# Rearranging the warm-up products and the first transposes at the start of a fused attention and GEGLU kernel

## The chip, the core and the metric

One core of one Trainium2 chip. The metric is device time in microseconds (us) for one execution.

## The reference

```python
scores = q @ k.T / sqrt(D) + alibi bias, causal, window 128     # B, H, S, D = 8, 8, 576, 64
attn   = softmax(scores) @ v                                    # 4608 tokens x 512
g, val = attn @ w_gate, attn @ w_val                            # 512 -> 1536
out    = (gelu(g) * val) @ w_out                                # 1536 -> 512
```

## The kernel before

Attention of batch 0 comes first. From then on TensorE runs dense products of the feed-forward part almost without a break, with the attention of the later batches between them. Only the start matters here. q and k of batch 0 come in a first part (320 tokens, four heads, then four more) and a tail (256 tokens). They are transposed on TensorE and copied out of PSUM, the buffer that TensorE writes to ("untangled"). Where TensorE would stand idle, `bank()` puts products of zeros ahead of the next real work. I read them as meant to bring its clock to full rate early: in the profile before, the clock record turns to full at 4.57 us, 3.37 after the first of them, and they start 0.43 us apart until then and 0.22 afterwards.

```python
    def bank():
        ps = psum.tile([128, 512], FP32, name="ps")
        for _ in range(heat.pop()):
            nc.tensor.matmul(out=ps, lhsT=zeros[:, 0:128], rhs=zeros, start=True, stop=True)
        ...
    load_runs(0, 0, 0, 4)                 # q, k: first part, heads 0 to 3
    zeros = consts.tile([128, 512], BF16, name="zeros")
    nc.vector.memset(zeros, 0.0)
    ...                                   # ident, tmpl
    load_runs(0, 0, 4, 8); load_runs(0, 1, 0, 8)      # heads 4 to 7; the tail
    load_v(0, (0, 1, 2)); load_w(0, 256); ...
    for h in range(H):                    # mask table, ScalarE
        nc.scalar.activation(out=emask[:, h, :], in_=tmpl, func=AF.Exp, scale=-slope)

    def first(cs):                        # c: a pair of heads; w: q or k
        for w in (0, 1):
            if w and len(cs) == 2:
                keep_busy(3)
            for c in cs:
                ps = bank().bitcast(BF16)
                transpose_runs(0, 0, w, c, ps)
                untangle(dve, 0, 0, w, c, ps)

    keep_busy(8)
    first((0, 1))
    made_later()
    keep_busy(4)
    scores(0, 0, (0, 1), lambda: (keep_busy(3), first((2,)), first((3,))))
    keep_busy(2)
    scores(0, 0, (2, 3))
    scores2(0)
    keep_busy(4); rest((0, 1)); keep_busy(1); rest((2, 3))   # transposes of the tail
    sums0(0)                              # 72 short products: row sums
    values_first(...)                     # products with v, spread, then xT
    ...                                   # scores of the tail, then dense products
```

The softmax here doesn't subtract the row's maximum and nothing guards it: scores larger than these inputs give would overflow.

## Time and profile before

| | before |
|---|---|
| median of the first three runs | 357.76 us (357.66 to 359.34) |
| median of six runs, with those beside the changed kernel | 358.23 us |
| span of the profiled run | 355.6 us |
| TensorE busy | 348.9 us, 98% |
| first dense product | 18.70 us |

### The profile page before, as it was taken

The page shows a single profiled execution, that of the slowest core. Times are in us where ns is not written, and L with a number is a line of the kernel's source. Part 1 is how long each engine was busy: PE and PEld are TensorE (multiplying, and loading weights), DVE is VectorE, ACT ScalarE, POOL GpSimd, SP SyncE. Part 2 cuts the span into 40 slices and gives each one's busy share as a digit, 9 for nine tenths or more (in the row PEclk, how much of TensorE's full clock was granted, in tenths as well). Part 3 has the DMA queues.
Part 4 walks back from the last instruction along what each step waited for, and adds up shares of the span by engine and source line. Part 5 has one row for each costly group of instructions (what it writes and reads, how often), then busy time and mean ns, then how long its engine had stood idle before and what let it go on. Part 6 is the DMA issues. An engine that isn't in the chain of part 4 may idle for free.

```text
span 355.6 us, 7101 instructions
## 1 busy us (share of the span) xinstructions
PE 348.9 (98%) x2869; PEld 174.6 (49%) x2869; DVE 188.3 (53%) x327; ACT 185.8 (52%) x342; POOL 103.1 (29%) x137
## 2 busy tenths in 40 slices
PE   8999999999999999999999999999999999999996
PEld 3667545444454445445444545454444444444443
DVE  4876578344988646646455554655474404403320
ACT  5884495536877375633873297337832233313322
POOL 8943479500940275003900192004000000000000
PEclk9999999999999999999999999999999999999999
DMA  7999999999999099983997399859206020011002
GB/s 93 182 195 197 202 160 193 148 154 166 141 157 174 12 185 180 158 177 41 153 208 151 78 133 200 142 129 98 88 4 133 32 88 1 2 68 50 2 29 88
DMA packets 145632, 42.62 MB, mean 120 GB/s; under 512 B 131608, under 2 KB 138520, under 8 KB 145600
## 3 DMA queue, kind: packets, MB, share of 16 engines
q0 software_dynamic: 106368, 18.88, 69.5%
q1 hardware_dynamic: 36432, 17.31, 22.2%
q10 hardware_dynamic: 2800, 5.99, 7.8%
q8 instruction: 22, 0.36, 0.4%
q14 instruction: 10, 0.08, 0.1%
HBM read 43.65 MB, written 9.53 MB: 150 GB/s over the span
## 4 chain that ended last, share of the span: by engine, by line
PE 94%; DVE 4%; issue 0%; ACT 0%; ACTq 0%; DVEq 0%
PE ps L392 53%; PE ps L415 25%; PE ps L358 5%; PE ps L190 4%; PE ps L70 2%; PE ps L315 2%; DVE P L200 1%; DVE r L321 1%; PE ps L151 1%; PE ps L429 1%; DVE kT L161 1%; PE ps L295 1%; PE ps L282 0%; PE ps L341 0%; DVE xT L379 0%
## 5 line engine op out<-in xcount | busy, mean ns | idle before, releaser
L399 DVE TENSOR_TENSOR hT<-ps,gelu 128x512 bf16<-128x512 f32 (+2 forms) x115 | 73.7, 653 | 105.8 <-PE ps L392 90.8
L398 ACT ACTIVATE gelu<-ps 128x512 bf16<-128x512 f32 (+2 forms) x115 | 65.1, 571 | 115.3 <-PE ps L392 111.5
L392 PE MATMUL ps<-xT,wg 128*128 128x512 bf16 (+2 forms) x460 | 112.3, 367 | 0.2
L392 PE MATMUL ps<-xT,wv 128*128 128x512 bf16 (+2 forms) x460 | 112.1, 366 | 0.0
L415 PE MATMUL ps<-wo,hT 128*128 128x512 bf16 x420 | 95.7, 380 | 0.0
L197 ACT ACTIVATE P<-ps 128x512 bf16<-128x512 f32 x144 | 73.1, 631 | 7.0 <-PE ps L190 7.0
L392 PEld LDWEIGHTS <-wv 128*128 128x128 bf16 x460 | 44.6, 98 | 48.8
L392 PEld LDWEIGHTS <-wg 128*128 128x128 bf16 x460 | 43.2, 98 | 47.4 <-issue 0.5
L200 DVE TENSOR_TENSOR P<-P,emask 128x1024 bf16<-128x1024 bf16 (+1 forms) x79 | 49.1, 641 | 30.1 <-ACT P L197 29.7
L415 PEld LDWEIGHTS <-hT 128*128 128x128 bf16 x420 | 38.9, 98 | 47.9 <-issue 3.7
L99 POOL DMA_DIRECT2D vb<-in_v_dram x40 | 33.9, 887 | 13.0 <-DMA ks<-in_k_dram 6.5
L420 ACT COPY osb<-ps 128x512 f32<-128x512 f32 x31 | 18.6, 601 | 32.8 <-PE ps L415 32.8
L621 POOL COPY mark<-hT 1x2 bf16<-1x2 bf16 x4 | 0.7, 174 | 95.0 <-DVE hT L399 95.0
L368 DVE TENSOR_TENSOR xT<-ps,rb 128x256 bf16<-128x256 f32 (+1 forms) x60 | 22.9, 443 | 9.2 <-DMA rb<-rd 4.7
L321 DVE RECIPROCAL r<-ps 128x320 f32<-128x320 f32 (+1 forms) x14 | 26.6, 1931 | 1.3 <-PE ps L315 1.3
L99 POOL DMA_DIRECT2D qs<-in_q_dram x30 | 25.2, 862 | 7.2 <-DMA wo<-in_moe_w_out_dram 5.1
L99 POOL DMA_DIRECT2D ks<-in_k_dram x30 | 25.4, 899 | 2.8 <-DMA qs<-in_q_dram 2.6
L190 PE MATMUL ps<-qT,kT 64*128 64x256 bf16 (+1 forms) x384 | 22.3, 244 | 1.4 <-DVE kT L161 0.6
L190 PEld LDWEIGHTS <-kT 64*128 64x128 bf16 x384 | 13.4, 94 | 13.6 <-issue 9.5
L358 PE MATMUL ps<-P,vb 128*64 128x128 bf16 (+2 forms) x384 | 18.1, 244 | 0.0
L358 PEld LDWEIGHTS <-vb 128*64 128x64 bf16 x384 | 14.7, 110 | 5.2 <-issue 4.8
L70 PE MATMUL ps<-zeros 128*128 128x512 bf16 x25 | 8.3, 460 | 1.2 <-DVE zeros L440 1.2
(73 smaller groups left out, 117.4 us busy)
## 6 DMA issues: line engine op xcount, KB each, us to landing
out_dram<-osb SPq DMA_DIRECT2D x35, 256.0 KB, 3.9
rb<-rd ACTq DMA_DIRECT2D x10, 576.0 KB, 7.4
vb<-in_v_dram POOLq DMA_DIRECT2D x32, 128.0 KB, 7.3
qs<-in_q_dram POOLq DMA_DIRECT2D x24, 128.0 KB, 6.2
ks<-in_k_dram POOLq DMA_DIRECT2D x24, 128.0 KB, 6.6
wo<-in_moe_w_out_dram POOLq DMA_DIRECT2D x2, 768.0 KB, 18.3
wg<-in_moe_w_gate_dram POOLq DMA_DIRECT2D x2, 384.0 KB, 9.2
wv<-in_moe_w_val_dram POOLq DMA_DIRECT2D x2, 384.0 KB, 10.7
```

The lines of the kernel that those rows point to most:

```text
L99: nc.gpsimd.dma_start(out=t[lo:128, j, :].rearrange("p (h d) -> p h d", h=H), in_=src[b][:, 128 * j - 64 + lo:128 * j + 64, :].rearrange(" ...
L190: nc.tensor.matmul(out=ps[:, col:col + 128 * n].rearrange("p (n t) -> p n t", n=n), lhsT=blocks(kT, b, i, c, j, 1).rearrange("p n t -> p ( ...
L197: nc.scalar.activation(out=dst, in_=src, func=AF.Exp, scale=0.125)
L200: nc.vector.tensor_tensor(out=dst, in0=dst, in1=m, op=ALU.mult)
L321: nc.vector.reciprocal(row(b)[:, lo:hi], ps[:, 0:hi - lo])
L358: nc.tensor.matmul(out=ps[64 * i:64 * i + 64, a:e], lhsT=vb[b % 2][:, j, 64 * h:64 * h + 64], rhs=prob(b, s, c, i, j, e - a), start=(j == ...
L368: nc.vector.tensor_tensor(out=xT[:, c, b * S + lo:b * S + hi], in0=ps[:, 0:hi - lo], in1=recip[b][:, c, lo:hi], op=ALU.mult)
L392: nc.tensor.matmul(out=ps[:, 0:hi - lo], lhsT=w[:, c, 128 * f:128 * (f + 1)], rhs=xT[:, c, t0 + lo:t0 + hi], start=(c == 0), stop=(c == 3))
L398: nc.scalar.activation(out=gl[:, 0:hi - lo], in_=pg[:, 0:hi - lo], func=AF.Gelu)
L399: nc.vector.tensor_tensor(out=hid[g][:, f, lo:hi], in0=pv[:, 0:hi - lo], in1=gl[:, 0:hi - lo], op=ALU.mult)
L415: nc.tensor.matmul(out=po, lhsT=hid[g][:, f, 128 * t:128 * (t + 1)], rhs=wo[:, f, :], start=(f == 0), stop=(f == NF - 1))
L420: (nc.vector.tensor_copy if g < 2 and t < 2 else nc.scalar.copy)(out=osb, in_=po)
```

## The change

Its intent: keep TensorE on products of zeros until k is about to land, then transpose q and k back to back; let ScalarE take one of the four first copies between the fifth and the sixth row of the mask table; and make zeros smaller, so that its memset ends earlier (it took 0.27 us in the profile before).

```diff
-            nc.tensor.matmul(out=ps, lhsT=zeros[:, 0:128], rhs=zeros, start=True, stop=True)
+            nc.tensor.matmul(out=ps.rearrange("p (n x) -> p n x", n=4), lhsT=zeros,
+                             rhs=zeros.unsqueeze(1).to_broadcast((128, 4, 128)),
+                             start=True, stop=True)
...
+    zeros = consts.tile([128, 128], BF16, name="zeros")
+    nc.vector.memset(zeros, 0.0)
     load_runs(0, 0, 0, 4)
-    zeros = consts.tile([128, 512], BF16, name="zeros")
-    nc.vector.memset(zeros, 0.0)
...
-    for h in range(H):
-        ...
+    make_emask(range(5))
...
-                keep_busy(3)
+                keep_busy(1)
...
-                untangle(dve, 0, 0, w, c, ps)
+                untangle(act if (w, c) == (0, 1) else dve, 0, 0, w, c, ps)
...
-    keep_busy(8)
+    keep_busy(11)
     first((0, 1))
+    make_emask(range(5, 8))
...
-    scores(0, 0, (0, 1), lambda: (keep_busy(3), first((2,)), first((3,))))
+    scores(0, 0, (0, 1), lambda: (keep_busy(2), first((2,)), first((3,))))
```

More of the change, by code (lines that the diff above doesn't have):

```diff
@@ L491, in made_last, with make_emask @@
         nc.vector.memset(vb[1][0:64, 0, :], 0.0)
-    for h in range(H):
-        slope = 2.0 ** (-8.0 * (h + 1) / H)
-        nc.scalar.activation(out=emask[:, h, :], in_=tmpl, func=AF.Exp, scale=-slope)
+    def make_emask(hs):
+        for h in hs:
+            slope = 2.0 ** (-8.0 * (h + 1) / H)
+            nc.scalar.activation(out=emask[:, h, :], in_=tmpl, func=AF.Exp, scale=-slope)
+    make_emask(range(5))
     act, dve = nc.scalar.copy, nc.vector.tensor_copy
```

## The prediction

> **What bounds the kernel now.** I read the page's busy table first, then the chain that ended last, then the order of time over the first 11 us, because every changed line runs there and nowhere else.
>
> ```profile
> PE 348.9 (98%) x2869; PEld 174.6 (49%) x2869; DVE 188.3 (53%) x327; ACT 185.8 (52%) x342; POOL 103.1 (29%) x137
> PE 94%; DVE 4%; issue 0%; ACT 0%; ACTq 0%; DVEq 0%
> ```
>
> TensorE is busy for 348.9 of 355.6 us and carries 94% of the chain. So whatever moves the start of the dense products (18.70 us, line 392) moves the end, and nothing else in this diff can. The busy table alone misleads at the start, where some of the work is products of zeros. The chain of waits up to there:
>
> ```profile
> 0.87 0.28 DVE zeros L440
> 1.16 0.05 issue
> 1.20 3.55 PE ps L70 x8
> 4.75 0.43 PE ps L151 x20
> 5.18 0.75 PE ps L70 x3
> 5.93 0.43 PE ps L151 x20
> 6.37 0.97 PE ps L70 x4
> 7.34 0.54 PE ps L190 x8
> 7.88 0.75 PE ps L70 x3
> 8.63 0.29 PE ps L151 x14
> 8.93 0.02 issue
> 8.95 0.49 DVE qT L161
> ```
>
> Line 70 is the product of zeros, line 151 the transposes, line 190 the scores. Up to 8.95 us the chain is TensorE from end to end, in program order: it waits for no transfer. From 8.95 to 10.65 us it is VectorE's four copies of the second half of q and k, then TensorE again. So a product of zeros ahead of 8.95 us is on the path, not beside it.
>
> The order of time shows the same place with real starts (the chain uses modelled ends):
>
> ```profile
> 4.68 0.50 PE L151 MATMUL ps<-ident,qs 64*64 64x64 bf16 x20
> 5.11 0.82 PE L70 MATMUL ps<-zeros 128*128 128x512 bf16 x3
> 5.86 0.50 PE L151 MATMUL ps<-ident,ks 64*64 64x64 bf16 x20
> 6.30 1.04 PE L70 MATMUL ps<-zeros 128*128 128x512 bf16 x4
> 7.27 0.61 PE L190 MATMUL ps<-qT,kT 64*128 64x256 bf16 x8
> ```
>
> Did k or the zeros hold the k transposes? The profile names the transfer of k as what ended the wait at 5.86. The transfer view gives 3.5 us from issue to landing for the first k load; issued at 1.99, it landed at 5.49 (the last landing record in the trace is 5.486). q, issued at 1.25 with 3.3 us, landed at 4.54. So k had lain there for 0.37 us; the three zeros (starts 5.11, 5.34, 5.55, the last ending 0.21 later at 5.77) held it, plus a gap of 0.09. The same 0.09 stands before q (eighth zero starts at 4.16, lasts 0.43, ends at 4.59; load at 4.68), before the scores (zeros end at 7.17, load at 7.26) and before the second transposes (8.25 + 0.21 = 8.47; 8.56). I count it as a fixed cost of a weight load that carries a wait, even one long satisfied.
>
> [...] starts 0.43 apart up to 4.16, 0.22 apart at 5.34 and 5.55, and the trace's clock record turns to full at 4.57, 3.37 after the first product. [...] the eight mask activations take 2.56 us in all, (2.56 - 0.40) / 7 = 0.31 apart. [...] the memset of zeros (256 words) took 0.27 us and that of ident (64 words) 0.11.
>
> **The change part by part.**
> The memset of zeros shrinks from 256 to 64 words: 0.27 to 0.11 us. It stays the first VectorE instruction, so TensorE starts at 1.04 instead of 1.20: -0.16. Moving it above the loads in the program changes the order on no engine.
>
> The products of zeros keep their 512 columns (128 columns read four times) and I assume their pace. Their number stays 25: 8+3+4+3 becomes 11+1+4+2 on the path, the rest is unchanged. Eleven from 1.04: first pitch 0.40, then 0.43, so the ninth starts at 4.43. If the clock turns 3.37 after the first product, the ninth to eleventh take 3 x 0.216 and end at 5.07; if it turns at 4.57 as before, 5.14. Add 0.09: q loads at 5.17 to 5.24 (landed since 4.54, so that wait is gone). The q transposes occupy 0.43 (4.68 to 5.11), then one zero 0.21: 5.81 to 5.88. Add 0.09: k at 5.91 to 5.98, against 5.86. So ahead of k the change is +0.05 to +0.12: one zero more (+0.21), less the earlier start, plus up to 0.07 if the clock doesn't follow.
>
> The scores follow k at the same distance (four zeros and 0.09), since the k copies still take VectorE 0.89 from 0.39 after the k transposes start and are covered. Scores at 7.32 to 7.39.
>
> The copy taken over by ScalarE: VectorE loses one of four early copies (0.45), but it sat idle 2.7 us before them and 0.30 between q and k. Those are off the path, worth 0. ScalarE finishes five mask activations at 3.96 + 5 x 0.31 = 5.5, waits for q's second transposes (about 5.24 + 0.35 + 0.18 = 5.8), copies 0.45 and makes three more masks: about 7.2. Its first exponential starts at 7.69 now, so it is free: worth 0.
>
> Behind the scores two zeros instead of three: -0.216. So the second transposes start at 8.56 + (0.05 to 0.12) - 0.22 = 8.39 to 8.46. The later half of k landed at 8.08, which still holds. VectorE idles 0.82 there, so its copies start earlier by the same amount, and so do scores, exponentials and masks.
>
> Sum on the path: -0.10 to -0.17, say -0.13 us. Is it kept to 18.70? The transfers in between leave room: the tail of k landed at 12.03 and is read at about 12.4, the third block of v at 14.23 for products from 14.55, the second gate piece at 18.85 for 20.9. So I take it as kept: 357.76 - 0.13 = 357.6.
>
> **The rivals.**
> First, the clock. [...] the eleven zeros all run cold, to 1.04 + 11 x 0.427 = 5.74, and everything after slips together. For it: one of the three timed runs took 359.34, 1.6 above the others[...]. It falls on both kernels[...]. Time 357.5 to 359.5.
> Second, VectorE or k was the true bound in usual runs, and the profiled one was lucky: then freeing a 0.45 us copy and placing q and k back to back gains up to 0.5: 357.2. Against it: 0.30 idle before the k copies, and k 0.37 early.
> Third, repeating columns streams slower, or a transfer absorbs the start (the third block of v has only 0.3 us to spare). Then 357.8.
> Fourth, ScalarE becomes the bound: a late q copy pushes the masks into the first exponential. It has 0.5 us of slack; 357.8 at worst.
>
> **Range and chances.** The whole affected stretch is under 9 us, 2.5% of the time; a change of 2% would have to remove 7 us. The runs differ by more (357.66 to 359.34) than the change is worth. Range 356.9 to 358.7, wide enough for the clock and the spread of chips. Faster by over 2%: 0.01; within 2%: 0.98; slower: 0.01.
>
> **What would show it.** Right: first product at about 1.04; eleven of zeros, the last two or three 0.22 apart; q transposes at about 5.2, k at 5.9 to 6.0; the copy on ScalarE between the fifth and sixth mask; scores at 7.3 to 7.4; second transposes at 8.4 to 8.5; line 392 first at about 18.6. Wrong: products of zeros slower than 0.22 when warm; k transposes ahead of 5.8; scores waiting for ScalarE; line 392 at 18.70 still, which would mean that something between absorbs the gain; or a median outside 356.9 to 358.7 with the clock turning at the same time.

The sum came to -0.10 to -0.17 us, of which -0.13 was named, and 357.76 - 0.13 = 357.6. Its paces stand in the profile before: zeros start 0.427 us apart before the clock's turn ("cold"; the first two 0.40) and 0.216 after it ("warm"; 0.23 for the first two of a group), masks 0.31 apart. That the clock turns 3.37 us after the first product again was my estimate from that one trace; the first rival is a later turn, with all eleven zeros cold (11 x 0.427, an estimate too). The 0.09 us that the sum adds for a load with a wait was measured at four places of that trace, such as 5.77 to 5.86 for k, which had landed at 5.49. All four loads are also of smaller tiles (64x64 or 64x128) than the zeros before them (128x128), and no run separates the two.

## More of the kernel before

The prediction shows the lines that carry its reading up to 9 us. The next ones decide this case. They are TensorE's part of the order of time (start, duration with modelled ends, engine, line, operation, out<-in, count) for the row sums, the products with v and the first dense products:

```profile
13.66 0.96 PE L282 MATMUL ps<-P,ones 128*32 128x80 bf16 x72
14.55 1.18 PE L358 MATMUL ps<-P,vb 128*64 128x192 bf16 x24
...
18.70 0.70 PE L392 MATMUL ps<-xT,wg 128*128 128x320 bf16 x4
```

All 72 row sums stand in one group without an idle note: in this execution nothing stopped them.

(The merged view notes no idle time where a stop is short; then only the length of the group gives it away, 0.96 us here.)

## The result, and the profile after

The changed kernel took 357.81 us in the median of six runs (357.52 to 358.58), before 358.23 (357.66 to 359.34). The ratio is 0.999 with a 95% interval of 0.9971 to 1.0009. Ratios here are the mean time of one kernel's fast runs over that of the other's in the same rounds, so not quite the ratio of the medians. That is "within 2%", and the time lies 0.2 us from the predicted one.

The profiled run of the changed kernel was its slowest (358.58 us). Its span is 356.8 us, 1.2 more than in the profile before. In the part that shows the chain that ended last, a transfer has appeared:

```profile
PE 91%; DVE 4%; DMA 2%; POOL 1%; issue 1%; ACT 0%; POOLq 0%; ACTq 0%; DVEq 0%
```

and followed in order of time, the chain no longer runs through the first products of zeros: it comes by way of a transfer:

```profile
6.04 7.23 DMA vb<-in_k_dram
13.28 0.04 issue
13.32 0.41 PE ps L153 x8
...
14.62 0.71 PE ps L284 x23
15.33 0.13 issue
15.46 0.36 PE ps L284 x7
```

The transfer is the tail of k (kept in a v tile that is free then). Line 284 is the row sums, and they are broken by a piece called "issue", which the first reading passed over. The order of time of the changed kernel (its lines are numbered two higher in this part):

```profile
1.00 4.42 PE L70 MATMUL ps<-zeros 128*128 128x512 bf16 x11 [1.00 <-DVE zeros L441]
5.36 0.50 PE L153 MATMUL ps<-ident,qs 64*64 64x64 bf16 x20
...
5.90 0.43 ACT L163 COPY qT<-ps 128x320 bf16<-128x320 bf16 x1 [0.29 <-PE ps L153]
6.11 0.50 PE L153 MATMUL ps<-ident,ks 64*64 64x64 bf16 x20
...
7.52 0.61 PE L192 MATMUL ps<-qT,kT 64*128 64x256 bf16 x8
...
13.32 0.41 PE L153 MATMUL ps<-ident,vb 128*64 128x128 bf16 x8 [0.67 <-DMA vb<-in_k_dram]
...
19.90 0.70 PE L394 MATMUL ps<-xT,wg 128*128 128x320 bf16 x4
```

The front does what the diff says: eleven zeros, the ScalarE copy in the gap of the mask table, k right after q. But TensorE then waits 0.67 us for the tail of k, which landed at 13.27 us (12.03 in the profile before), and the first dense product is at 19.90 instead of 18.70: exactly the 1.2 us of the spans. So at first sight 1.2 us of landing decided this profile, ten times what the change was predicted to be worth; the experiments correct that reading. The question became: what decides when the dense products start, and is the change's gain there at all?

### The profile page after: what moved, and what is told of

It reads as the page before. It is cut to its first block, busy times and chain, and to the rows that moved or that the text cites. A ratio compares the mean times of both kernels' runs of the same rounds, so it can differ in the third digit from the quotient of the medians.

```text
span 356.8 us, 7101 instructions
## 1 busy us (share of the span) xinstructions
PE 349.4 (98%) x2869; PEld 175.1 (49%) x2869; DVE 187.9 (53%) x326; ACT 186.5 (52%) x343; POOL 103.3 (29%) x137
## 4 chain that ended last, share of the span: by engine, by line
PE 91%; DVE 4%; DMA 2%; POOL 1%; issue 1%; ACT 0%; POOLq 0%; ACTq 0%; DVEq 0%
PE ps L394 53%; PE ps L417 25%; PE ps L360 5%; PE ps L192 4%; DMA vb<-in_k_dram 2%; PE ps L317 2%; DVE P L202 1%; DVE r L323 1%; PE ps L431 1%; PE ps L153 1%; PE ps L284 1%; PE ps L297 1%; PE ps L343 0%; POOL ks L128 0%; DVE kT L163 0%
## 5 line engine op out<-in xcount | busy, mean ns | idle before, releaser
L360 PEld LDWEIGHTS <-vb 128*64 128x64 bf16 x384 | 14.7, 110 | 5.2 <-issue 4.8
```

Source lines behind the costliest of these rows:

```text
L360: nc.tensor.matmul(out=ps[64 * i:64 * i + 64, a:e], lhsT=vb[b % 2][:, j, 64 * h:64 * h + 64], rhs=prob(b, s, c, i, j, e - a), start=(j == ...
```

## The experiments

Twelve runs, each with runs of the kernel before on the same chip. I held two theories at first, **path** (TensorE's own order, as in the prediction) and **tail** (landings of the tail of k and of v), and formed a third on the way.

### before_again, after_again: both kernels once more

No edit.

> The kernel before against itself, to see what the times scatter by and to get a second trace of it. Theory 'tail' (the landing of the tail of k, not TensorE's own order, decides when the dense products start, and that landing scatters by over 1 us): ratio 1.000, single times spread over 357.5 to 359.3, and in its trace the second group of tail transposes starts 0.05 us after the tail of k lands whenever that is later than about 12.4 us. Theory 'path' (TensorE's order alone): the dense products start at 18.7 again, within 0.1 us.

> The changed kernel again, with more rounds. Theory 'path': 0.13 us faster than before plus or minus the clock's turning (0.9996). Theory 'tail': between 0 and -0.1 us on average, hidden in the scatter; the second transposes start at 8.4 to 8.6 us, depending on when the clock turns, and the dense products start at the landing of the tail of k plus 6.6 us if that is later than 12.4 us.

Before against itself: 1.000 (0.998 to 1.002), six runs from 357.52 to 359.61. The changed kernel: 1.0006 (0.9988 to 1.0023), 357.58 to 359.14. The means were 358.45 (before, eleven runs), 358.40 and 358.44. So the change is worth nothing that these runs can see.

The trace of before_again starts its dense products at 19.91, against 18.70 for the same program, and not for the tail of k (landed at 12.45). Its row sums show where it stopped:

```profile
13.73 0.78 PE L282 MATMUL ps<-P,ones 128*32 128x80 bf16 x62
15.48 0.36 PE L282 MATMUL ps<-P,ones 128*32 128x48 bf16 x10 [0.97 <-issue]
```

TensorE stands still for 0.97 us in the middle of 72 equal short products, after the 62nd, and the profile names "issue": it waited for nothing that the profile shows. Counted from the start of the program, the product that waits is TensorE's 224th.

The trace of after_again shows no such stop, and yet no gain at the dense products:

```profile
12.05 0.96 PE L153 MATMUL ps<-ident,vb 128*64 128x128 bf16 x16
...
13.83 0.96 PE L284 MATMUL ps<-P,ones 128*32 128x80 bf16 x72
...
18.87 0.70 PE L394 MATMUL ps<-xT,wg 128*128 128x320 bf16 x4
```

The first transposes of the tail start 0.16 us earlier than in the profile before (12.21), but take 0.96 us instead of 0.64: the tail of k landed at 12.55, and TensorE's weight loads waited 0.29 us for it. So here the tail alone used up the gain; the dense products start 0.17 us later than in the profile before (19.15 by the rule that I had written for 'tail').

### before_no_zeros_second, after_six_zeros_second: a zero more or less

```diff
-    scores(0, 0, (0, 1), lambda: (keep_busy(3), first((2,)), first((3,))))     # before
+    scores(0, 0, (0, 1), lambda: (first((2,)), first((3,))))
-    scores(0, 0, (0, 1), lambda: (keep_busy(2), first((2,)), first((3,))))     # changed
+    scores(0, 0, (0, 1), lambda: (keep_busy(6), first((2,)), first((3,))))
```

> The kernel before without the three products of zeros ahead of the second transposes (the change takes one of them out). Theory 'path': three times 0.216 us off the path, -0.65 us, ratio 0.9982, unless the later half of k (landing at 8.1 us) or the start of the transposes holds it: then at least -0.35 us. Theory 'tail': the transposes and scores start 0.4 to 0.6 us earlier in the trace, but the tail's transposes still start when the tail of k lands, and the time changes by 0 to -0.2 us.

> The changed kernel with six products of zeros instead of two ahead of the second transposes: 4 x 0.216 = 0.86 us more work in TensorE's order. Theory 'path': 0.86 us slower than the changed kernel, ratio to before about 1.002. Theory 'tail': as much as the landing of the tail leaves is hidden; at a landing of 13.3 us (as in the profiled run of the changed kernel) all of it, at 12.0 us all but 0.2 to 0.4; on average +0.3 to +0.6 us.

Without three zeros: 0.9994 (0.9979 to 1.0008), mean 358.19, 0.26 us below before; 'path' had asked for at least 0.35, and the interval holds both. With four more: 1.0031 (1.0015 to 1.0047), mean 359.52, 1.1 us above the changed kernel, where 0.86 was the most that either theory had. In its one trace the clock turned only at 7.03 us, 6.0 after the first product, so all eleven zeros ran at the slow pace (the last four took 1.91 us, where four after the turn take 1.04) and the q transposes took 0.74 us instead of 0.50; that may be the rest, but 0.2 us is within the scatter of six runs. The row sums of the two kernels:

```profile
14.26 0.81 PE L282 MATMUL ps<-P,ones 128*32 128x80 bf16 x65
15.76 0.30 PE L282 MATMUL ps<-P,ones 128*32 128x80 bf16 x7 [0.69 <-issue]
```

```profile
15.47 0.75 PE L284 MATMUL ps<-P,ones 128*32 128x80 bf16 x58
16.46 0.43 PE L284 MATMUL ps<-P,ones 128*32 128x48 bf16 x14 [0.25 <-issue]
```

Three products fewer ahead, and the stop comes three row sums later (65 instead of 62); four more ahead, and it comes four earlier (58). It is tied to a number of instructions, not to a piece of work or a time. That is what made the third theory, **fetch**: TensorE runs out of instructions. The traces hold one 16 KB packet on the instruction queue in this stretch (called the fetch below), of 0.95 to 1.2 us, at 11.65 us in the profile before and at 12.92 in before_again. The page of the profile before counts 22 packets on this queue, and 5738 instructions of TensorE (2869 weight loads and as many products); the kernel with 66 more (after_short_zeros, below) has 23. So I took the packets to bring TensorE's instructions, about 261 each, or 130 products (an estimate, 5738 / 22), and reckoned with 128: the stop at the 224th product then belongs to a block that begins there, and the one before it begins at the 96th, which serves as a mark below. No view shows whose instructions a packet brings or where a block begins; a later stop, ahead of the 351st product (after_short_zeros), lies 127 products behind the 224th.

### before_front_only, after_front_only: no landings in the way

The loads of the tail and of v are left out and their tiles cleared by VectorE. The result is wrong.

```diff
-    load_runs(0, 1, 0, 8)
-    load_v(0, (0, 1, 2))
     load_w(0, 256)
...
-    nc.vector.memset(vb[0][0:64, 0, :], 0.0)
+    nc.vector.memset(vb[0][:, 0:3, :], 0.0)
+    nc.vector.memset(vb[1][:, 1:5, :], 0.0)
```

> A wrong result on purpose: the kernel before without the loads of the tail of q and k and of the first three blocks of v of batch 0 (VectorE clears those tiles instead), so that no landing after 8.1 us can hold the start. Theory 'path' (TensorE's order sets the start even with the loads): same time as before, 358.3 on the same chip. Theory 'tail' (the landings of the tail of k and of v hold the start in most runs): about 0.7 us faster on average, dense products at 18.6 to 18.7 us in the trace, and the single times lie within 0.4 us of each other, where those of before spread over 1.5 us.

> The same for the changed kernel; also wrong on purpose. With the landings gone the front is TensorE and VectorE alone, so this tests the prediction's sum: 0.10 to 0.17 us faster than the same kernel made from before (0 to 0.2 where the clock turns later), dense products at 18.5 to 18.6 us. If the sum is wrong (repeated columns slow, the ScalarE copy late), equal or slower.

0.9994 (0.9982 to 1.0006) and 1.0004 (0.9991 to 1.0016); means 358.08 and 358.43 against 358.36. So 'tail' falls as the main cause: with those landings taken away, only 0.28 us of the expected 0.7 came for before, inside the scatter, and dense products started at 19.37 and 20.40. A part it may have: the single times of before_front_only lie within 0.55 us (0.4 was expected), those of before in the same call within 1.3, though of five runs against eleven. The stop was still there, here in the second kernel:

```profile
14.60 0.78 PE L284 MATMUL ps<-P,ones 128*32 128x80 bf16 x62
15.97 0.36 PE L284 MATMUL ps<-P,ones 128*32 128x48 bf16 x10 [0.59 <-issue]
```

The pair doesn't test the prediction's sum: in the profile of after_front_only the clock turned 6.0 us after the first product, in the other 3.1.

### after_short_zeros: move the stop

```diff
-        for _ in range(heat.pop()):
-            nc.tensor.matmul(...128x512...)
+        n = heat.pop()
+        for x in range(4 * n if n == 11 else 0):      # 44 products of 128 columns
+            lo = 128 * (x % 4)
+            nc.tensor.matmul(out=ps[:, lo:lo + 128], lhsT=zeros, rhs=zeros,
+                             start=True, stop=True)
+        for _ in range(0 if n == 11 else n):
+            nc.tensor.matmul(...)
```

> The changed kernel with the first eleven products of zeros cut into 44 of 128 columns, the same time on TensorE but 33 more pairs of instructions[...]. Theory 'fetch' (the 16 KB instruction fetch, 0.95 us[...], sits at 11.6 to 13.4 us in the traces and makes v land late when it falls after 12.5): the fetch moves to 9 to 10.5 us, the third block of v lands at 14.0 to 14.7 us, mean time 0.4 to 0.7 us below before. Theory 'scatter elsewhere' (the fetch has no part in it): v lands anywhere from 14.0 to 16.2 us and the time equals the changed kernel's.

1.0009 (0.9997 to 1.0021), mean 358.62: my hope of 0.4 to 0.7 us less did not come, but the fetch moved, as 'fetch' says. It came at 8.46 us (9 to 10.5 was expected), 0.7 us after the 96th product, the stop in the row sums was gone (all 72 in one group), dense products began at 19.10 with 0.29 us of waiting for the tail of k, and a stop turned up later, among the dense products:

```profile
19.10 0.70 PE L399 MATMUL ps<-xT,wg 128*128 128x320 bf16 x4
20.23 0.70 PE L399 MATMUL ps<-xT,wv 128*128 128x320 bf16 x4 [0.43 <-issue]
```

That is ahead of the 351st product, one short of 224 + 128 = 352; instructions that the trace doesn't list could account for the one, which is not shown. The second fetch had run from 17.87 to 18.83 us, so TensorE went on 1.40 us after its end. The 33 products more moved the stall in this trace; they didn't remove it. The variant of the expectation in which v's landing was the link is also wrong: v's third block landed at 14.95, outside the 14.0 to 14.7 that I had written.

### before_quiet, after_quiet: an idle DMA system while the fetch is due

Like the two front-only kernels, and the weights are issued only once the second half of k is copied. Wrong, too.

```diff
+    nc.gpsimd.tensor_copy(out=mark, in_=by_pair(kT[0])[0:1, 3, 64:66])
     load_w(0, 256)
     load_w(256, 640)
     ...                           # all moved behind the second transposes
```

> Wrong result on purpose: like the kernel before without the landings of the tails and of v, and with the weight loads held back until the second half of k is copied (about 10.6 us), so that the DMA engines stand idle from 8.1 to about 12 us. Theory 'fetch starves TensorE' (in all traces so far TensorE stops only ahead of its 224th product, and goes on 1.3 to 1.5 us after a 16 KB instruction fetch has ended[...]): the fetch starts within 1 us of the 96th product, by 10 us, the gap ahead of the 224th product is gone, dense products at 18.5 to 18.7 us, mean time 357.4 to 357.7, single times within 0.5 us of each other. If the fetch has nothing to do with it: a gap of 0.6 to 1.2 us stays ahead of the 224th product, and the time stays at 358.0 to 358.3.

When the packet is asked for and what it waits for, no view shows; in the traces up to then it started 0.7 to 4.8 us after the 96th product.

> The same made from the changed kernel; wrong on purpose. With no landing and no starving the front is TensorE and VectorE alone: the prediction's sum says 0.10 to 0.17 us faster than the same kernel made from before where the clock turns at the same time after the first product, dense products at 18.4 to 18.6 us. A clock that turns at 7 us (as in two of the eight traces with eleven zeros or so) makes it up to 1 us slower instead.

The transfer view of 8 to 16 us in 40 slices of 0.2 us: busy tenths of the DMA engines, and what they moved. First before_again, then before_quiet:

```profile
DMA  9999999999999999999999999999999999999999
GB/s 99 136 151 154 163 169 159 166 179 175 161 148 171 168 160 164 156 158 156 157 154 157 151 149 227 154 159 158 154 164 188 182 191 200 194 187 198 197 201 204
```

```profile
DMA  0000000004000000000000029889999999999999
GB/s 0 0 0 0 0 0 0 0 0 82 0 0 0 0 0 0 0 0 0 0 0 0 0 28 84 56 61 151 197 172 200 200 187 190 202 195 182 177 182 144
```

The 16 KB packet is the 227 in the 25th slice of the first (12.8 to 13.0 us) and the lone 82 in the tenth slice of the second (9.8 to 10.0). With nothing in its way it starts 0.9 us after the 96th product (1.4 in after_quiet), where it took 2.8 to 4.8 us under load in the traces tabulated below (0.7 in after_short_zeros, where that product started at 7.74 us). And the stop is gone. TensorE's row sums and first dense products of before_quiet, then of after_quiet:

```profile
13.71 0.96 PE L282 MATMUL ps<-P,ones 128*32 128x80 bf16 x72
...
18.75 0.70 PE L392 MATMUL ps<-xT,wg 128*128 128x320 bf16 x4
```

```profile
13.50 0.96 PE L284 MATMUL ps<-P,ones 128*32 128x80 bf16 x72
...
18.54 0.70 PE L394 MATMUL ps<-xT,wg 128*128 128x320 bf16 x4
...
22.50 0.72 PE L394 MATMUL ps<-xT,wv 128*128 128x320 bf16 x4 [1.09 <-DMA wv<-in_moe_w_val_dram]
```

The times don't show it: 1.0017 (1.0002 to 1.0032) and 1.0001 (0.9987 to 1.0014), because the weights that I held back now arrive late (the last line; 1.16 us in the other kernel): span minus the start of the dense products is 0.8 to 0.9 us more than in the plain kernels. My expectation of 357.4 to 357.7, with single times within 0.5 us, overlooked that (1.4 us in before_quiet). Against each other, the two kernels differ by 0.58 us on average in the change's favour, but five runs each don't set that apart from chance (95% interval about 0 to 1.2 us), and the starts differ by less. The start is the measure here: 18.54 against 18.75, with the clock turning 3.4 and 3.5 us after the first product, 0.21 us earlier for the change, with one trace of each.

### The order of the tail transposes

```diff
-    rest((0, 1)); keep_busy(1); rest((2, 3))           # each: q, then k
+    rest(0, (0, 1)); rest(0, (2, 3)); keep_busy(1); rest(1, (0, 1)); rest(1, (2, 3))
```

It reads k's tail later. I tried it on the changed kernel, and when it came out fastest of all, on both.

> The changed kernel with the tail transposes in another order: both groups of q first, then the zero, then both groups of k, so k's tail is read about 0.6 us later. Theory 'tail of k holds it': 0.2 to 0.6 us faster than the changed kernel on average. Theory 'v holds it' (the third block of v lands last and the products need it whatever the tail does): no change in time, 0 plus or minus 0.2; dense products start at the landing of v's third block plus 4.0 to 4.1 us when that is over 14.6 us.

> The kernel before with the order of the tail transposes that ran 0.13% faster on the changed kernel (both groups of q, then both of k). If that gain was the wait for k's tail: also 0.1 to 0.5 us faster than before here. If it was chance, or the fetch alone decides: 0 plus or minus 0.3 us.

> The changed kernel with the tail transposes reordered, again, beside the same reordering of before. Under 'fetch starves TensorE' the change is worth nothing beside it: the two reordered kernels within 0.3 us of each other. Under the prediction's sum: 0.13 us faster. In its trace the gap, if any, stands ahead of the 224th product, and products go on 1.3 to 1.5 us after the fetch ends.

On the changed kernel 0.9987 (0.9971 to 1.0003) the first time and 1.0012 (0.9996 to 1.0027) the second; on before 1.0008 (0.9994 to 1.0023). The first gain was scatter, and the two reordered kernels lie 0.17 us apart (358.42 and 358.59). 'v holds it' fails too: the first reordered trace starts its dense products at 19.33, where its rule gives 18.9 to 19.0 (v's third block landed at 14.94). The repeat shows the longest stop of all: 1.4 us between the 223rd and the 224th product, dense products at 20.94. No kernel beats the two reliably.

### What the traces say together

| trace | clock full, after first product | 96th product | fetch | 224th product, gap before it | after fetch's end |
|---|---|---|---|---|---|
| before | 3.4 | 8.84 | 11.65 to 12.60 | 14.25, none | 1.7 |
| before_again | 2.9 | 8.82 | 12.92 to 14.09 | 15.48, 1.17 | 1.39 |
| before_no_zeros_second | 3.1 | 8.59 | 13.41 to 14.45 | 15.76, 0.89 | 1.31 |
| before_front_only | 3.1 | 8.74 | 12.69 to 13.67 | 14.93, 0.79 | 1.27 |
| before_quiet | 3.5 | 8.89 | 9.81 to 11.27 | 14.32, none | 3.1 |
| after | 3.8 | 8.87 | 13.04 to 13.99 | 15.46, 0.33 | 1.47 |
| after_again | 3.5 | 8.68 | 11.61 to 12.56 | 14.42, none | 1.9 |
| after_six_zeros_second | 6.0 | 10.61 | 14.24 to 15.19 | 16.46, 0.45 | 1.27 |
| after_front_only | 6.0 | 9.77 | 13.65 to 14.60 | 15.96, 0.79 | 1.37 |
| after_k_tail_last | 4.6 | 9.25 | 12.63 to 13.59 | 14.89, 0.24 | 1.30 |
| after_k_tail_last_2 | 5.8 | 9.71 | 14.22 to 15.20 | 16.51, 1.40 | 1.31 |
| after_quiet | 3.4 | 8.68 | 10.05 to 10.98 | 14.09, none | 3.1 |

Gaps are from start to start, times in us. Two traces are left out: after_short_zeros, whose stop lies elsewhere, and before_k_tail_last, where records of products are missing. Weight loads are all recorded, and in before_k_tail_last they tell the same: they stop for 0.35 us behind the 224th and go on at 15.16, 1.32 us after the end of the fetch (12.85 to 13.84). before_quiet, after_quiet and after_k_tail_last_2 also lack some 40 of 2869 products; the weight loads put their 96th within 0.04 us of the table and the 224th of the quiet pair within 0.06; in after_k_tail_last_2 they, too, stop behind the 224th. Where there is a gap, TensorE goes on 1.27 to 1.47 us after the fetch has ended, whatever it is doing; where the fetch was early enough there is none. The gap of 0.2 to 1.4 us is there in eight of the twelve, and the packet took 0.93 to 1.5 us. At three later places in the profile before, 128 products apart, there is next to nothing: the 352nd, 480th and 608th products start at most 0.08 us after the one ahead. In all six traces of before, changed and the two kernels with other numbers of zeros, span minus the start of the dense products is 336.9 us. So all that distinguishes these profiled runs happens before the dense products.

## Why the prediction was right or wrong

**The verdict and the range held**: 0.999 with an interval around 1, and 357.81 us in 356.9 to 358.7. That tests the sum little: before itself, at 358.23, lies in the range, so it would have held without any gain, and the third rival's figure, 357.8, is nearer than the 357.6 that was named. Single runs scatter by more than these differ.

**What bounds the front: incomplete.** "It waits for no transfer" was said of the first 8.95 us of the one trace I had, and I took it for a rule for the whole start. The kernel's start has a second limit, the fetch: where there is a gap, the 224th product starts 1.27 to 1.47 us after its end. The first trace met it with no visible gap (the fetch had come early, at 11.65 us). The view of the DMA queues listed the instruction queue with 22 packets, and I passed over it. The 1.6 us spread of the three timed runs may have been the sign of it: I gave that to the clock alone.

**The memset and the start: right**, 0.11 us and the first product at 1.00 (predicted 1.04).

**The sum of the front: right where the clock turns as before.** In after_again (clock at 3.5) q came at 5.17, k at 5.93, scores at 7.33, second transposes at 8.41: all inside the predicted 5.17 to 5.24, 5.91 to 5.98, 7.32 to 7.39 and 8.39 to 8.46. The gain at the 96th product is 0.14 to 0.16 us against the two traces of before, and about 0.2 in the quiet pair (predicted 0.10 to 0.17; before_quiet's q transposes started 0.05 later than before's; its q landed at 4.64 instead of 4.54 and its clock turned only after the eighth zero, and which of the two it was is open). Products with repeated columns keep their pace: 0.427 and 0.216 us from start to start in the profile of the changed kernel. The copy on ScalarE ran at 5.90 for 0.43 us, between the fifth and sixth mask, and the first exponential at 7.94 waited 0.69 us for TensorE: off the path, as predicted.

**The clock: too narrow.** I allowed 0.07 us for it. After the first product it turned at 2.9 to 6.0 us in these traces. In the profile of the changed kernel it came at 3.8, which made the ninth zero cold (0.43 us to the next one, 0.26 in after_again) and q late (5.36), and at 6.0 the second transposes are about 1 us late. Of six traces with eight zeros first, one turned later than 4.5 us after the first product, of eight with eleven (short or long), four. Whether the change makes a late turn likelier stays open: so few traces don't tell it from chance.

**"So I take it as kept": this step failed.** I checked three landings in one trace and found room. Two waits took it. The tail of k, read about 0.4 us after its landing in that trace, was waited for in the profiled run (0.67 us) and in after_again (0.29 us, with no other stop). Behind it comes the fetch: in no tabulated trace does the 224th product start less than 1.27 us after its end. In the profiled run the fetch ended at 13.99, so even with the tail in time the 224th product would have started at 15.26 at the earliest instead of 15.46 (an estimate, with the least delay of the table, 1.27 us): most of the 1.2 us would have been lost without the late tail. The fetch starts 2.8 to 4.8 us after the 96th product under load, a scatter of 2 us behind a gain of 0.13. The quiet pair shows the other side, in one trace each: with the fetch early, the stop is absent and the dense products start 0.21 us sooner with the change. With the loads in place, two sets of rounds show ratios of 0.999 and 1.0006, with intervals of about plus or minus 0.6 us; whether a part of the 0.13 us is kept on average, these can't tell. The fourth rival, ScalarE, and the second, VectorE, did not show; the third, a transfer, did, but the transfer that the stops follow was mainly the packet on the instruction queue, which no rival named.

What is shown: the stop's place follows the instruction count (58, 62, 65 row sums; 127 products later with 33 more products ahead), its end follows the fetch, and it was absent in all four tabulated traces in which the fetch had ended by 12.6 us, two of them made early on purpose. Not shown, and only my reading: that TensorE's instructions are what it brings and that it is asked for at the 96th product (count and place fit, no view shows it), and that it waits behind data packets (it starts 0.9 and 1.4 us after that product with idle DMA engines and 2.8 to 4.8 under load, but I could see no single engine's queue). Nor is it shown why the tail of k came 1.2 us late in the one trace, where a single 256-byte packet took 1.37 us instead of 0.04.

## What to carry to other kernels

A gain ahead of a wait that scatters need not arrive: before adding up a front, look at how much the single runs differ, and find the step that differs. In a stretch of very short instructions, count them: here the stops lay ahead of the 224th and the 351st product, 127 products or 254 recorded instructions apart, and with the DMA engines busy TensorE stood for 0.2 to 1.4 us with "issue" as the only trace. Removing or adding a few instructions only moved the stop here (58, 62 or 65 row sums before it); what counted was the time from the 96th product to the 224th (5.4 us in the profile before, from 8.84 to 14.25), against up to 4.8 us until the packet starts, about 1.0 of transfer and 1.3 until TensorE goes on.
